# Lean tail scores for two more pairs, one matmul group moved behind its slot's unit, one decode half moved behind the tail's maximum

## The chip, the cores and the metric

The kernel runs on one core of one Trainium2 chip. The metric is the device time of one execution in microseconds. The engines are TensorE (PE; its weight loads are listed apart as PEld), VectorE (DVE), ScalarE (ACT), GpSimd (POOL) and SyncE (SP, which issues DMAs here).

## The reference

Attention with a multiplicative decay, then a mixing layer with a low-rank token mix and a feed-forward block, all in float32, for 8 batches, 8 heads, 576 tokens and 64 columns per head:

```
scores = scale * q @ k^T
cum    = cumsum(log(clip(f, 1e-4, 1)), axis=-1)
scores = where(causal, -1e9, scores + cum[:, None] - cum[None, :])
attn   = softmax(scores)            # max subtracted, sum + 1e-9
x      = attn @ v                   # heads put side by side: (8, 576, 512)
h      = x^T @ U @ V                # rank 32, over tokens
u      = x + h^T
out    = u + relu(u @ w1) @ w2      # 512 -> 2048 -> 512
```

## The kernel before

The work is cut into 32 pairs of heads (four pairs a batch) that run through a pipeline of steps. Step t has ten slots. In its slots TensorE does, in an order written out in the function `step`: the scores of pair t, the transposes of the exponentials and the value products of pair t-1, and the last value products, output transposes and rank products of pair t-2. Each slot can also take one unit of a filler list. In the step in which a batch's fourth pair is done, the units are those of the mix (`mix_units`: H, Tu, Tv); in the others they are the first half of the feed-forward block (`ffn_units`: A is a group of 12 matmuls, B of 6). After about 690 us only the second half of the feed-forward block is left.

The scores of one head of a pair are four blocks of 128 rows, S_00 to S_03 and S_10 to S_13 (head, block). The last 64 tokens of both heads are done together as "the tail", in two halves of 288 columns, St_0 and St_1 (`score_tail`). Each score goes through the same chain: TensorE writes it into a bank of PSUM, VectorE takes the masked row maximum (L439, for the tail L477), ScalarE takes the exponential out of the bank (L449, for the tail L487, named Ptl). A later score is put in the same bank, so it waits for that exponential. Pairs 0 to 5 work on plain float32 operands (L415); pairs 6 to 31 on operands that are split in two parts (L418, L419, L472, L473), which ScalarE and GpSimd make for the next pair (G, L339 to L359).

`ranks` (L715) makes Tt, nine small matmuls on the outputs xh and xl of pair t-2. It takes a bank of a pool of two, T, shared with the transposes T_10, T_11, T_12. From Tt ScalarE makes two copies (L718, L719) and VectorE one difference (L722). The outputs' split xh, xl is made on ScalarE and GpSimd (L699, L700, L701).

The feed-forward weights arrive in a packed form and are decoded piece by piece in the first steps by `decode` and `decode_words` (L76 to L93, on VectorE and ScalarE). From piece 12 on (`LATE`) a piece is decoded in two halves, and the second half is put behind a named instruction by `behind`: an order on VectorE without a wait.

In steps 1 to 6 only TensorE's order is written by hand, from step 7 on SP's too; a scheduler orders VectorE, ScalarE and GpSimd. `defer(phase, fn, n)` hands a function to the slot n slots later. `NO` is the first pair whose tail takes the mask with the decay already in it (`load_tail` L368, `lean_mask` L382), and `NF` the first with split operands. With both at 6, `join_tail` (L377, L378) never ran.

Of the kernel before, what the change touches and what calls it, by code (L numbers as in the profile page):

```python
# [36 lines left out]
NG = B + 1  # L37
NX = 3
NF = 6
NO = 6  # L40


@with_exitstack
def tile_decay_attention_moe(ctx, tc, qk, v, f, U, V, w1, w2, out):
    nc = tc.nc
# [9 lines left out]
    newest = {}  # L55

    def behind(ins, kind):
        found = newest[kind]
        for x in found if isinstance(found, tuple) else (found,):
            tc.add_manual_dep(  # L60
                ins.ins, x.ins.name,
                mybir.DependencyInfo(mybir.DependencyClass.NoSync, mybir.DependencyReason.DATA), reason=f"order behind {kind}",
            )

    def decode(raw, a, h, l, eng, rows=slice(0, 128), keep=False, sub=nc.gpsimd, low=None, halves=(0, 1)):

        lo, hi = raw[..., 0].bitcast(U32), raw[..., 1]
        af, gf = a.bitcast(F32), hi.bitcast(F32)
        if 0 in halves:
            decode_words(a, af, hi, gf, eng, keep)
        if 1 in halves:
            third = nc.vector.tensor_scalar(hi, a, -0x800000, None, op0=ALU.bitwise_and)  # L76
            if 0 not in halves:
                behind(third, "top")
            nc.vector.scalar_tensor_tensor(gf, lo, 2.0**-52, gf, op0=ALU.mult, op1=ALU.mult)
            sub.tensor_tensor(af, af, gf, op=ALU.add)  # L80
            nc.scalar.copy(h, af)
            (low or sub).tensor_tensor(l[rows], af[rows], h.bitcast(F32)[rows], op=ALU.subtract)

    def decode_words(a, af, hi, gf, eng, keep):

        if eng is nc.scalar:
            first = nc.scalar.mul(af, gf, 2.0**-112)
        else:
            first = eng.tensor_scalar(af, gf, 2.0**-112, None, op0=ALU.mult)
        if keep:  # L90
            tc.keep_in_program_order(first)
        nc.vector.tensor_scalar(hi, hi, -0x80000000, None, op0=ALU.bitwise_and)
        nc.vector.scalar_tensor_tensor(a, a, 3, hi, op0=ALU.logical_shift_left, op1=ALU.bitwise_or)  # L93
# [156 lines left out]
    def decode_w(u, halves=(0, 1)):  # L250
        load_w(u)
        raw, a = staged[u]
        if 1 in halves:
            staged[u] = None
        kind, fc = UNITS[u]
        if kind == "w1":
            h, l = (x[:, fc].rearrange("p c f -> p (c f)") for x in (w1h, w1l))
        elif kind == "w2":
            h, l = w2h[:, fc], w2l[:, fc]
        elif kind == "V":  # L260
            h, l = VV, VV
        else:
            raw = raw.rearrange("p (c r) t -> p c r t", c=NM + 1)
            a = a.rearrange("p (c r) -> p c r", c=NM + 1)
            h, l = Us[:, :, 0:RK], Us[:, :, RK : 2 * RK]
        decode(raw, a, h, l, nc.scalar, slice(96, 128) if kind == "V" else slice(0, 128), keep=True, sub=nc.vector if u not in (0, LATE) else nc.gpsimd, low=nc.vector if 0 < u < LATE else nc.gpsimd, halves=halves)
        if u == len(UNITS) - 1 and 1 in halves:
            nc.gpsimd.memset(xn[NX - 1][64:128, NM, :], 0.0)

# [7 lines left out]
    def defer(phase, fn, slots=1):  # L277
        later.setdefault(now[0] + slots, []).append((phase, fn))
# [6 lines left out]
    def run_filler():  # L285
        w, fn = filler.pop(0)
        fn()
        return w
# [73 lines left out]
    def load_tail(p):  # L362

        if not NO <= p < NP:
            return
# [4 lines left out]
    def join_tail(p):  # L370

        if not NO <= p < NF:
            return
# [6 lines left out]
    def lean_mask(p):  # L380
        if NO <= p < NP:
            nc.gpsimd.tensor_tensor(lean[:, MAIN:S], lean[:, MAIN:S], tri, op=ALU.add)  # L382
# [40 lines left out]
    def bank_s(p, name):  # L423

        scored[0] += 1
        if p < NF and scored[0] % 2:
            return psF.tile([P, 512], F32, tag="F", name=name)
        return psS.tile([P, 512], F32, tag="S", name=name)
# [31 lines left out]
    def score_tail(p, x):  # L460
        z = st[p]
        ps = bank_s(p, f"St{p}_{x}")
        cols = slice(hw * x, hw * x + hw)
        if p < NO:
            for j in range(2):
                qk_mm(ps[:, :hw], p, ATAIL[j], cols, j == 0, j == 1, j)
        elif p < NF:
            nc.tensor.matmul(ps[:, :hw], both_q, both_k[:, cols], start=True, stop=True)
        else:
            at = [slice(AOFF[j] + cols.start, AOFF[j] + cols.stop) for j in range(2)]  # L470
            for j in range(2):
                nc.tensor.matmul(ps[:, :hw], G[j][:, 0, ATAIL[j] : ATAIL[j] + P], G[j][:, 2, at[j]], start=j == 0, stop=False)  # L472
            nc.tensor.matmul(ps[:, :hw], G[1][:, 1, 0:P], G[1][:, 3, at[1]], start=False, stop=True)  # L473
        z["tl"].append(ps)

        def top():
            nc.vector.tensor_tensor_reduce(  # L477
                ps[:, :hw], ps[:, :hw], lean[:, hw * x : hw * x + hw], scale=-SCALE,
                scalar=3.0e38 if x == 0 else z["nm"][:, 8:9],
                op0=ALU.add, op1=ALU.min, accum_out=z["nm"][:, 8 + x : 9 + x],  # L480
            )

        def use():
            if x == 1:
                z["ptl"] = sb.tile([P, S], F32, tag="Ptl", name=f"Ptl{p}")
                for y in range(2):
                    newest["tail"] = nc.scalar.activation(  # L487
                        z["ptl"][:, hw * y : hw * y + hw], z["tl"][y][:, :hw], AF.Exp, bias=z["nm"][:, 9:10],
                        scale=-1.0, accum_out=z["sm"][:, 8 + y : 9 + y],
                    )  # L490

        defer(0, top)
        defer(2, use)
# [211 lines left out]
    def ranks(p):  # L705
        z = st[p]
        b, hp = z["b"], z["hp"]
        if hp == 0:
            TSb[b] = sf.tile([P, DM], F32R, tag="TS", name=f"TS{b}")
        TS = TSb[b]  # L710
        fs = slice(P * hp, P * hp + P)
        tp = psT.tile([P, 512], F32, tag="T", name=f"Tt{p}")
        for i in range(NM + 1):
            for x in (z["xh"], z["xl"])[: 2 if i < NM else 1]:
                nc.tensor.matmul(tp[0:64, 0:P], Us[:, i], x[:, i], start=i == 0 and x is z["xh"], stop=i == NM)  # L715


        defer(1, lambda: nc.scalar.copy(TS[0:64, fs], tp[0:64, 0:P]))  # L718
        defer(1, lambda: nc.scalar.copy(TS[96:128, fs], tp[0:32, 0:P]))  # L719
        defer(  # L720
            4,
            lambda: nc.vector.tensor_tensor(  # L722
                TS[64:96, fs], tp[0:32, 0:P], TS.bitcast(F32)[0:32, fs], op=ALU.subtract
            ),
        )
# [208 lines left out]
    LATE = 12  # L934
# [7 lines left out]
    def step(t):  # L942
        p = SEQ[t]
        a, c = (SEQ[t - x] if t >= x else None for x in (1, 2))
        ps_, pa, px = p is not None, a is not None, c is not None
        last, ending = t == LAST, t > LAST - 2
# [7 lines left out]
        for s in range(6 + 2 if last else SLOTS):  # L954
# [35 lines left out]
            if (t, s) in DECODES:  # L990
                u = DECODES.index((t, s))

                steps = [lambda: load_w(u + (3 if u < 6 else 2)), lambda: decode_w(u)]
                if u < LATE:
                    for fn in steps if u < 8 else steps[::-1]:
                        at(6, fn)
                else:
                    at(6, lambda: decode_w(u, (0,)))
                    defer(6, lambda: decode_w(u, (1,)), 3)
                    defer(6, steps[0], 3)  # L1000
            run_later()
            if s == 4 and ps_ and p > NF:
# [30 lines left out]
                turn_p(a, 1, s - 6)  # L1033
            if pa and s == 7:
                values(a, 0)
            if px and s == (6 if last else 8):
                ranks(c)

            if mixing:
                for _ in range(2 if t == MIX[0] and s < 3 else 1):  # L1040
                    mixing.pop(0)[1]()
                for _ in range(1 if ending else (1, 1, 2, 1, 1)[s] if s < 5 else 0):
                    if filler:
                        run_filler()
            elif len(filler) > held(t) and s in ROOM:

                ahead = sum(x >= s for x in ROOM) + len(ROOM) * (min(m for m in MIX if m > t) - 1 - t)
                credit[0] += (len(filler) - held(t)) / max(ahead, 1)
                if credit[0] > 0.999 or t > LAST - 3:
                    credit[0] = max(credit[0] - 1, 0)  # L1050
                    run_filler()
            if ps_ and s == 6:
                score(p, 1, 0)
            if last and s == 7:
# [114 lines left out]
    with tc.manual_schedule(engines={ET.PE, ET.DVE, ET.Activation, ET.SP}):  # L1169
# [12 lines left out]
        h, t = ([fn for _, fn in x] for x in (mixing[0 : NM + 1], mixing[NM + 1 :]))  # L1182
# [622 lines left out]
```

## Time and profile before

| | |
|---|---|
| time, median of 3 executions | 1185.39 us (1185.22 to 1187.29) |
| the profiled execution, its own time | 1184.63 us |
| its span, first to last instruction | 1182.9 us |
| TensorE's mean granted clock | 0.999 |
| busy: PE, PEld | 1168.8 us, 1074.3 us |
| busy: DVE, ACT, POOL | 903.0 us, 752.7 us, 594.2 us |

The span is what the views of the trace add up to. About 1.7 us of the execution's own time lie around it. The median of the three timed executions is 0.76 us above the profiled one.

### The profile page before, as it was taken

How to read it: one execution, taken by the hardware profiler on the slowest of the kernel's cores; microseconds unless marked ns; L12 is line 12 of the kernel's file. 1: busy time of each engine (PE TensorE's matmuls, PEld its weight loads, DVE VectorE, ACT ScalarE, POOL GpSimd, SP SyncE). 2: the span in 40 equal slices, each digit the busy share in tenths (PEclk: the TensorE clock that was granted, in tenths of full speed). 3: DMA queues.
4: the chain of work that ended last, by engine and by line, in shares of the span. 5: the costliest groups of instructions: out<-in, count | busy, mean ns of one | idle time of the engine just before them, and what ended most of it. 6: DMA issues, size and time to landing. Idle time of an engine off the chain costs nothing.

```text
span 1182.9 us, 24145 instructions
## 1 busy us (share of the span) xinstructions
PE 1168.8 (99%) x8348; PEld 1074.3 (91%) x8348; DVE 903.0 (76%) x2185; ACT 752.7 (64%) x2046; POOL 594.2 (50%) x668
## 2 busy tenths in 40 slices
PE   9999999999999999999999999999999999999998
PEld 5888899899999989989989987798999999999998
DVE  8987787677777677777686799967776767777675
ACT  8878786766868668867765577344454544544443
POOL 4216766547648458666563000024575555555554
PEclk9999999999999999999999999999999999999999
DMA  5754545536536536546443155352325335243411
GB/s 159 205 151 135 149 121 163 147 98 171 141 98 183 151 86 178 135 112 178 108 129 111 70 163 182 109 143 98 100 90 141 93 124 143 90 117 99 131 49 36
DMA packets 90610, 150.47 MB, mean 127 GB/s; under 512 B 12888, under 2 KB 50264, under 8 KB 88440
## 3 DMA queue, kind: packets, MB, share of 16 engines
q1 hardware_dynamic: 88856, 140.14, 40.4%
q0 software_dynamic: 1152, 8.39, 3.8%
q8 instruction: 66, 1.08, 0.4%
q14 instruction: 56, 0.46, 0.1%
q10 hardware_dynamic: 480, 0.40, 0.1%
HBM read 108.64 MB, written 35.93 MB: 122 GB/s over the span
## 4 chain that ended last, share of the span: by engine, by line
PE 85%; DVE 9%; ACT 3%; issue 1%; DMA 1%; POOL 1%; SPq 0%; DVEq 0%; POOLq 0%; ACTq 0%
PE N L1416 12%; PE B L854 11%; PE A L832 11%; PE A L1396 9%; PE B L1396 7%; PE V L642 6%; PE T L530 4%; PE S L418 3%; PE S L419 2%; PE O L1497 2%; PE B L1416 2%; PE V L607 2%; PE S L415 2%; PE Tt L715 2%; PE O L1260 1%
## 5 line engine op out<-in xcount | busy, mean ns | idle before, releaser
L208 POOL TENSOR_TENSOR hb<-xn,hb 128x256 fp32r<-128x256 f32 x136 | 111.6, 841 | 125.5 <-ACT hb L203 112.9
L449 ACT ACTIVATE P<-S,nm 128x128 f32<-128x128 f32 (+3 forms) x256 | 137.5, 539 | 58.0 <-DVE nm L439 56.0
L439 DVE CUSTOM_DVE_ANT_0 S<-S,mask 128x128 f32<-128x128 f32 (+3 forms) x256 | 125.4, 494 | 52.3 <-PE S L419 41.5
L832 PE MATMUL A<-uh,w1h 128*128 128x256 f32 (+1 forms) x384 | 119.7, 312 | 0.0
L832 PE MATMUL A<-ul,w1h 128*128 128x256 f32 (+1 forms) x384 | 113.6, 296 | 0.0
L832 PE MATMUL A<-uh,w1l 128*128 128x256 f32 (+1 forms) x384 | 113.4, 295 | 0.0
L203 ACT CAST hb<-xn 128x256 fp32r<-128x256 f32 x136 | 51.7, 404 | 84.6 <-DVE xn L1402 45.5
L339 POOL CAST G<-qk 64x576 fp32r<-64x576 f32 (+1 forms) x76 | 50.1, 668 | 89.2 <-PE S L419 56.8
L854 PE MATMUL B<-w2h,hh 128*128 128x512 f32 x216 | 88.2, 408 | 0.0
L509 DVE TENSOR_TENSOR PTl<-T,PTh 128x512 fp32r<-128x512 f32 (+1 forms) x156 | 78.1, 526 | 10.3 <-ACT PTh L506 9.9
L530 PE MATMUL T<-ident,P 128*128 128x128 f32 x544 | 85.3, 272 | 0.0
L854 PE MATMUL B<-w2l,hh 128*128 128x512 f32 x216 | 84.9, 393 | 0.0
L854 PE MATMUL B<-w2h,hl 128*128 128x512 f32 x216 | 84.7, 392 | 0.0
L358 POOL TENSOR_TENSOR G<-qk,G 64x576 fp32r<-64x576 f32 x52 | 74.7, 1437 | 10.8 <-issue 3.8
L1416 PE MATMUL N<-sw,hb 128*128 128x256 f32 x546 | 79.9, 282 | 0.0
L1416 PE MATMUL N<-b2h,hb 128*128 128x256 f32 x420 | 79.8, 282 | 0.0
L359 POOL TENSOR_TENSOR G<-qk,G 64x576 fp32r<-64x576 f32 x52 | 74.9, 1441 | 8.4 <-ACT G L339 7.5
L832 PEld LDWEIGHTS A<-uh,w1h 128*128 128x128 f32 x384 | 72.8, 190 | 0.9 <-DVE hl L837 0.4
L832 PEld LDWEIGHTS A<-uh,w1l 128*128 128x128 f32 x384 | 73.0, 190 | 0.5
L418 PE MATMUL S<-G 128*128 128x128 f32 x208 | 71.4, 348 | 2.0 <-ACT Ptl L487 0.9
L832 PEld LDWEIGHTS A<-ul,w1h 128*128 128x128 f32 x384 | 72.7, 189 | 0.0
L1416 PEld LDWEIGHTS N<-sw,hb 128*128 128x128 f32 x546 | 71.6, 190 | 0.0
(349 smaller groups left out, 3992.6 us busy)
## 6 DMA issues: line engine op xcount, KB each, us to landing
qk<-in_qk_dram SPq DMA_DIRECT2D x104, 288.0 KB
direct<-ud SPq DMA_DIRECT2D x48, 256.0 KB
sr<-in_w_dram SPq DMA_DIRECT2D x20, 512.0 KB
vr<-in_v_dram SPq DMA_DIRECT2D x32, 256.0 KB
ud<-uh SPq DMA_DIRECT2D x32, 256.0 KB
ud<-ul SPq DMA_DIRECT2D x32, 256.0 KB
accd<-ost SPq DMA_DIRECT2D x32, 256.0 KB
xn<-accd SPq DMA_DIRECT2D x8, 1024.0 KB
```

What stands on the lines that cost most here:

```text
L208: return leng.tensor_tensor(dl, src, dh.bitcast(F32), op=ALU.subtract)
L358: low = pin(el.tensor_tensor(g[oth, 2, cols], k[oth], gf[oth, 2, cols], op=ALU.subtract))
L359: last = pin(em.tensor_tensor(g[own, 1, cols], q[own], gf[own, 0, cols], op=ALU.subtract))
L418: nc.tensor.matmul(ps, G[j][:, 0, c0 : c0 + P], G[j][:, 2, cols], start=first, stop=False)
L439: ins = newest["top"] = nc.vector.tensor_tensor_reduce(ps[:, :w], ps[:, :w], mask[:, 512 - w : 512], scale=-SCALE, scalar=3.0e38, op0=ALU. ...
L449: ins = nc.scalar.activation(pt, ps[:, :w], AF.Exp, bias=z["nm"][:, col : col + 1], scale=-1.0, accum_out=z["sm"][:, col : col + 1])
L509: defer(2, lambda: nc.vector.tensor_tensor(dstl, src, dsth.bitcast(F32), op=ALU.subtract))
L530: nc.tensor.transpose(tp[:, P * x : P * x + P], z["P"][j][i][:, P * c : P * c + P], ident)
L832: nc.tensor.matmul(ps[:, :nt], wt[:, fc, c], ut[:, c, sl], start=m == 0, stop=m == 3 * NDC - 1)
L854: nc.tensor.matmul(ps, ht[:, fc, P * x : P * x + P], wt[:, fc], start=fc == 0 and m == 0, stop=fc == NA - 1 and m == 2,)
L1396: nc.tensor.matmul(ps, a[x][:, c], b[y][:, c], start=start and m == 0, stop=m == 5, skip_group_check=not start)
L1416: nc.tensor.matmul(ps[:, y], a[p_][:, P * y : P * y + P], w[q_], start=start and y == 0 and m == 0, stop=stop and y == 1 and m == 2,)
```

## The change

Three edits stand in the diff. `NO` goes from 6 to 4, so the tails of pairs 4 and 5 are one float32 matmul a half (L468, on both heads' operands side by side, `both_q` and `both_k`) in place of two (L415); GpSimd copies those operands (L377, L378), two DMAs a pair bring the mask's rows (L368) and GpSimd adds the triangle (L382). `ranks` goes from in front of slot 8's unit to behind it, in all steps but the last. The second half of the decoding of piece 13, in step 7, is deferred five slots rather than three, and is ordered behind the tail's maximum (`newest["low"]`, L477) rather than the newest maximum of a main score (`top`, L439).

```diff
-NO = 6
+NO = 4
...
-    def decode(raw, a, h, l, eng, rows=slice(0, 128), keep=False, sub=nc.gpsimd, low=None, halves=(0, 1)):
+    def decode(raw, a, h, l, eng, rows=slice(0, 128), keep=False, sub=nc.gpsimd, low=None, halves=(0, 1), after="top"):
...
             third = nc.vector.tensor_scalar(hi, a, -0x800000, None, op0=ALU.bitwise_and)
             if 0 not in halves:
-                behind(third, "top")
+                behind(third, after)
...
-        decode(raw, a, h, l, nc.scalar, slice(96, 128) if kind == "V" else slice(0, 128), keep=True, sub=nc.vector if u not in (0, LATE) else nc.gpsimd, low=nc.vector if 0 < u < LATE else nc.gpsimd, halves=halves)
+        decode(raw, a, h, l, nc.scalar, slice(96, 128) if kind == "V" else slice(0, 128), keep=True, sub=nc.vector if u not in (0, LATE) else nc.gpsimd, low=nc.vector if 0 < u < LATE else nc.gpsimd, halves=halves, after="top" if u == LATE else "low")
...
         def top():
-            nc.vector.tensor_tensor_reduce(
+            newest["low"] = nc.vector.tensor_tensor_reduce(
                 ps[:, :hw], ps[:, :hw], lean[:, hw * x : hw * x + hw], scale=-SCALE,
...
-                    defer(6, lambda: decode_w(u, (1,)), 3)
+                    defer(6, lambda: decode_w(u, (1,)), 3 if u == LATE else 5)
...
-            if px and s == (6 if last else 8):
+            if px and last and s == 6:
                 ranks(c)
...
                     credit[0] = max(credit[0] - 1, 0)
                     run_filler()
+            if px and not last and s == 8:
+                ranks(c)
             if ps_ and s == 6:
                 score(p, 1, 0)
```

On TensorE, slot 8 of step 15 stood so before (a name ends in its tile's number; A_0_5 is the slot's unit, of which the first and the last matmul are shown):

```order
L530 MATMUL T_12_4143<-ident,P_13_3879 128x128 x2
L715 MATMUL Tt_4147<-xh_4032,Us 64x128
L715 MATMUL Tt_4147<-xl_4033,Us 64x128
...
L832 MATMUL A_0_5_4157<-uh_3738,w1h 128x256
...
L418 MATMUL S_13_4187<-G_92 128x512
```

and so in the changed kernel:

```order
L530 MATMUL T_12_4153<-ident,P_13_3889 128x128 x2
L832 MATMUL A_0_5_4157<-uh_3748,w1h 128x256
...
L832 MATMUL A_0_5_4157<-ul_3749,w1h 128x256
L715 MATMUL Tt_4170<-xh_4042,Us 64x128
L715 MATMUL Tt_4170<-xl_4043,Us 64x128
...
L418 MATMUL S_13_4197<-G_92 128x512
```

Tt is now the last thing in front of the score S_13. On VectorE, in the same slot, the unit's difference (L837) stands now in front of Tt's (L722), which is still the last in front of S_13's maximum. The rows of the changed kernel:

```order
L509 TENSOR_TENSOR PTl_3919<-T_12_4153,PTh_3918 128x128
L837 SCALAR_TENSOR_TENSOR hl_0_3942<-A_0_5_4157,hh_0_3941 128x256
L722 TENSOR_TENSOR TS_3846<-Tt_4170,TS_3846 32x128
L439 ISA S_13_4197,nm_3883<-S_13_4197,mask 128x512
L439 ISA nm_3883 128x1
```

On VectorE in step 7, around the tail's second maximum, before (L76, L79 and L80 are the decode half):

```order
L477 ISA St_0_1606,nm_1474<-St_0_1606,mask 128x288
L76 TENSOR_SCALAR xn_109<-stg_1079 128x512
L837 SCALAR_TENSOR_TENSOR hl_0_1457<-A_0_2_1578,hh_0_1456 128x256
L580 TENSOR_TENSOR PT_1508<-Ty_None,PT_1508 64x128
L79 SCALAR_TENSOR_TENSOR xn_109<-xn_109 128x512
L477 ISA St_1_1637,nm_1474<-St_1_1637,mask,nm_1474 128x288
L837 SCALAR_TENSOR_TENSOR hl_0_1457<-A_0_3_1612,hh_0_1456 128x256
L80 TENSOR_TENSOR stg_1079<-stg_1079,xn_109 128x512
L509 TENSOR_TENSOR PTl_1507<-T_v,PTh_1506 128x2x2x64 x2
L509 TENSOR_TENSOR PTl_1507<-T_10_1664,PTh_1506 128x512
L439 ISA S_10_1682,nm_1474<-S_10_1682,mask 128x128
```

and in the changed kernel:

```order
L477 ISA St_0_1610,nm_1484<-St_0_1610,mask 128x288
L837 SCALAR_TENSOR_TENSOR hl_0_1467<-A_0_2_1588,hh_0_1466 128x256
L580 TENSOR_TENSOR PT_1518<-Ty_None,PT_1518 64x128
L477 ISA St_1_1641,nm_1484<-St_1_1641,mask,nm_1484 128x288
L76 TENSOR_SCALAR xn_109<-stg_1091 128x512
L837 SCALAR_TENSOR_TENSOR hl_0_1467<-A_0_3_1616,hh_0_1466 128x256
L79 SCALAR_TENSOR_TENSOR xn_109<-xn_109 128x512
L509 TENSOR_TENSOR PTl_1517<-T_v,PTh_1516 128x2x2x64 x2
L80 TENSOR_TENSOR stg_1091<-stg_1091,xn_109 128x512
L439 ISA S_10_1692,nm_1484<-S_10_1692,mask 128x128
```

The maximum of St_1 has passed L76 and L79, and the first differences of PTl and S_10's maximum have moved with it. On GpSimd, at the end of step 2 and in step 3 (a + is a row that is only there after, a - one that stood there before; qk_98 and qk_99 are the operands of pair 4):

```order
 L701 TENSOR_TENSOR xl_552<-xn_107,xh_551 128x512
+L377 COPY both_q<-qk_98 64x64
+L378 COPY both_k<-qk_98 64x576
 L521 MEMSET PT_671 64x128
-L700 TENSOR_TENSOR xh_738<-xn_107,xh_738 64x128
-L701 TENSOR_TENSOR xl_739<-xn_107,xh_738 128x512
+L377 COPY both_q<-qk_99 64x64
+L378 COPY both_k<-qk_99 64x576
 L154 MEMSET G_91 64x576
...
+L700 TENSOR_TENSOR xh_738<-xn_107,xh_738 64x128
+L701 TENSOR_TENSOR xl_739<-xn_107,xh_738 128x512
+L382 TENSOR_TENSOR mask<-mask,tri 128x64
```

The second half of xh and xl (L700, L701), which Tt of step 3 reads, stands now behind two copies that need the load of qk_99, and behind five memsets.

## Rows read from the trace of the kernel before

**Rows 1.** The page: busy time of each engine, and the chain by engine

```profile
...
PE 1168.8 (99%) x8348; PEld 1074.3 (91%) x8348; DVE 903.0 (76%) x2185; ACT 752.7 (64%) x2046; POOL 594.2 (50%) x668
...
PE 85%; DVE 9%; ACT 3%; issue 1%; DMA 1%; POOL 1%; SPq 0%; DVEq 0%; POOLq 0%; ACTq 0%
```

**Rows 2.** Waits of TensorE's weight loads: us, times, longest

```profile
...
PEld S L418 <- ACT Ptl L487: 3.5, 15, 1.1
...
PEld Tt L715 <- DVE PTl L509: 3.4, 11, 0.5
```

**Rows 3.** Fp32 tail scores of pairs 0 to 5, by form

```profile
...
L415 PE MATMUL St<-qk 128*128 128x288 f32 x48 | 13.4, 411 | 0.1
```

**Rows 4.** Timeline of step 4, TensorE and ScalarE (start, duration, engine, line)

```profile
...
68.69 1.14 PE L415 MATMUL St<-qk 128*128 128x288 f32 x4
...
70.54 0.82 PE L415 MATMUL S<-qk 128*128 128x128 f32 x4
...
70.25 0.26 ACT L449 ACTIVATION_READ_ACCUMULATOR P<-S,nm 128x1 f32 x1
```

**Rows 5.** Timeline of step 5, the same two engines

```profile
...
85.67 0.82 PE L415 MATMUL S<-qk 128*128 128x128 f32 x4
...
84.62 0.23 ACT L449 ACTIVATION_READ_ACCUMULATOR P<-S,nm 128x1 f32 x1
```

**Rows 6.** Timeline of step 3: a DMA issue, GpSimd, and Tt

```profile
...
50.52 1.18 SPq L307 DMA_DIRECT2D qk<-in_qk_dram  x2
...
51.77 0.45 POOL L700 TENSOR_TENSOR xh<-xn,xh 64x128 fp32r<-64x128 f32 x1 [6.84 <-ACT xh L699]
...
55.62 0.20 POOL L158 MEMSET G<- 128x128 f32 x1
...
60.64 0.30 PE L715 MATMUL Tt<-xh,Us 128*64 128x128 f32 x1
```

**Rows 7.** A later mask row: its DMA issue and GpSimd's use of it

```profile
...
103.38 1.14 SPq L368 DMA_DIRECT2D mask<-based  x2
...
107.14 0.32 POOL L382 TENSOR_TENSOR mask<-mask,tri 128x64 f32<-128x64 f32 x1 [0.53 <-DMA mask<-based]
```

**Rows 8.** Timeline of step 7: GpSimd, VectorE, TensorE's loads

```profile
...
122.19 1.77 POOL L208 TENSOR_TENSOR VS<-vr,VS 128x640 fp32r<-128x640 f32 x1
...
123.21 1.29 DVE L79 SCALAR_TENSOR_TENSOR xn<-xn 128x512 f32<-128x512 uint32 x1
...
124.43 0.51 DVE L477 CUSTOM_DVE_ANT_0 St<-St,mask,nm 128x288 f32<-128x288 f32 x1
...
125.67 0.19 PEld L418 LDWEIGHTS S<-G 128*128 128x128 f32 x1 [1.10 <-ACT Ptl L487]
...
128.82 0.44 PE L418 MATMUL S<-G 128*128 128x384 f32 x1 [0.36 <-ACT P L449]
```

**Rows 9.** The same line 79 in step 4

```profile
...
71.38 0.69 DVE L79 SCALAR_TENSOR_TENSOR xn<-xn 128x512 f32<-128x512 uint32 x1
```

**Rows 10.** Two of the waits of line 715's weight loads

```profile
...
191.33 0.13 PEld L715 LDWEIGHTS Tt<-xh,Us 128*64 128x64 f32 x1 [0.22 <-DVE PTl L509]
...
298.22 0.13 PEld L715 LDWEIGHTS Tt<-xh,Us 128*64 128x64 f32 x1 [0.52 <-DVE PTl L509]
```

**Rows 11.** End of step 15 and start of step 16

```profile
...
300.25 0.28 DVE L722 TENSOR_TENSOR TS<-Tt,TS 32x128 fp32r<-32x128 f32 x1 [0.26 <-ACT TS L719]
...
302.51 0.19 ACT L449 ACTIVATION_READ_ACCUMULATOR P<-S,nm 128x1 f32 x1
...
302.80 0.36 PE L418 MATMUL S<-G 128*128 128x256 f32 x1
```

**Rows 12.** End of step 10, in which a batch is mixed

```profile
...
193.63 0.59 ACT L755 COPY full<-Tu 128x512 f32<-128x512 f32 x1
...
195.25 0.19 ACT L449 ACTIVATION_READ_ACCUMULATOR P<-S,nm 128x1 f32 x1
...
195.49 0.39 PE L418 MATMUL S<-G 128*128 128x256 f32 x1
```


## The prediction

> **What bounds the kernel now.** I read the page first. TensorE is busy for 1168.8 of 1182.9 us, and the chain that ended last runs over it for 85% [rows 1]. So a gain is either TensorE work taken out or one of its idle stretches closed, and those sum to only 14.1 us. The next view is the list of waits of TensorE's weight loads, which is where a stalled TensorE shows: a matmul's load stands still before the matmul does. Two of its longest entries are touched by the diff: line 418 waiting for the exponentials Ptl (3.5 us in 15 places, the longest 1.1) and line 715 waiting for VectorE's difference PTl (3.4 us in 11 places) [rows 2]. Then I looked at the timeline around each place, to see which release would end last once the listed one is gone. That second release decides this change, because most PSUM banks are handed on with a few tenths of a us to spare.
>
> **Lean tails of pairs 4 and 5.** A tail half before is two float32 matmuls, which the trace records as four rows; a row takes 0.41 us alone [rows 3], and four in a run take 1.14 us, so one follows another after (1.14 - 0.41) / 3 = 0.24 us [rows 4]. A lean half is one matmul, two rows: 0.49 us less. Four halves make 1.95 us at most. The trace has no row of line 468; its operands have the same kind and width as those of the tail rows, so I take their spacing.
>
> How much of it stays is read from the score behind the tails. In step 4 the group of S_10 and S_11 starts at 70.54, while ScalarE finishes the exponential that S_11's bank waits for (that of S_03) at 70.25 + 0.26 = 70.51 [rows 4]. S_11 comes some 0.2 us into its group, so TensorE can come only about 0.2 us earlier before it waits there. I keep 0.2 of 0.97. In step 5 the same exponential is done at 84.62 + 0.23 = 84.85 and the group starts at 85.67 [rows 5], so S_11 has about 1.0 us of room: I keep 0.9, a little under the whole, since the scheduler moves one ScalarE copy in front. The sum is -1.1 us, the bounds -0.2 (both steps held by ScalarE) and -1.95.
>
> What the edit adds is off TensorE: four GpSimd copies and one mask add a pair, and two DMA issues a pair of 0.57 us each on SP [rows 7]. I cost it at nothing because of slack on GpSimd, with one tight place. In step 3 the copies of qk_99 now stand in front of five memsets and of L700 and L701. That load's issue ends at 51.70 [rows 6]. The nearest DMA with a visible consumer, a mask row, was used 107.14 - 104.52 = 2.6 us after its issue [rows 7], so the copies start near 54.3. The two copies I put at 0.45 (a 128-column operation on 64 partitions, [rows 6]) and 0.9 (half of the two-input operation of 640 columns, 1.77, [rows 8]); the block from L700 to the last memset took 55.82 - 51.77 = 4.05 us [rows 6]. This ends at 59.7, and Tt of step 3, which reads xl, starts at 60.64 [rows 6]: 0.9 us to spare. With a copy of the full 1.77 it is just used up, and each further 0.1 us of delay costs 0.1 us.
>
> The row of line 79 in step 7 shows what GpSimd can do to VectorE: 1.29 us with a GpSimd operation running from 122.19 to 123.96 [rows 8], 0.69 us for the same shape in step 4 with none [rows 9]. The Trainium skill, SBUF — State Buffer, section Who interferes with whom, says that a VectorE instruction with two SBUF inputs and a GpSimd instruction that reads SBUF exclude each other and that the second one waits for the first to finish. The trace agrees in size: 1.29 is 0.60 more, and GpSimd's operation ended 0.75 us after line 79 began. By that rule the new copies would hold up decode instructions of steps 3 to 5 by up to a copy each; what they delay is decoding and the tail's exponentials, whose banks are taken over two scores after S_11, so the sum would stay as it is.
>
> **The decode half in step 7.** Before, VectorE works on L79 from 123.21, and the tail's second maximum starts only at 124.43; its exponential then lets S_10 go at 125.67, after 1.10 us of waiting [rows 8]. In the new order the maximum passes L76 and L79, so it can start at 123.2, 1.2 us earlier. S_10 would then wait for almost nothing: at most 1.1 us is gained. The work does not go away, it stands behind: S_10's maximum now follows L79, the first PTl differences and L80, and S_12 takes the bank of S_10's exponential, which it already waits for at 128.82 [rows 8]. In the new order S_10's maximum has passed one difference, PTl of T_10 (about 0.7 us), and has been passed by none, but ScalarE has the G casts in front of that exponential. I put the gain that reaches S_12 at 0.5 us, between 0 (the old wait moves to S_12 whole) and 1.1.
>
> **Tt behind the unit.** Tt's bank is that of T_11, so Tt waits until VectorE has read T_11. With a unit in between (0.4 to 1.5 us of TensorE work) that wait is over, which is 3.4 us in 11 places [rows 2]: six steps that mix a batch with 0.22 each (1.3 us in all, as at 191.33), and five with a feed-forward unit (0.26, three of 0.52, as at 298.22, and 0.22; 2.0 us) [rows 10]. But now Tt's evacuation runs right in front of S_13's maximum: on ScalarE two copies, on VectorE L722 with 0.28 us [rows 11]. So the exponential of S_13 comes about 0.28 us later against TensorE than before, and its bank is the one that S_01 of the next step needs. At the end of step 15 that exponential is done at 302.51 + 0.19 = 302.70, and S_01 starts at 302.80 [rows 11]: there 0.52 us can be closed in front, and about 0.3 is kept, as it is at the other such place (step 23). The remaining three with a feed-forward unit have over a microsecond of room at S_01 and keep all, 1.0 us together. Kept: 1.6 us.
>
> In the six mixing steps S_01 already follows the exponential at 0.05 us (195.25 + 0.19 = 195.44 against 195.49) [rows 12]. There the gain of 0.22 ends at S_01 in any case, and what counts is when the exponential comes. The copy of the fourth Tu (0.59 us, [rows 12]) moves in front of the exponential of S_12, and everything behind it up to L722 and S_13's maximum comes about 0.1 us later, so I book +0.1 six times, +0.6. One more step (step 8, no wait before, 0.1 us of room at S_01) I book at +0.1. The other moved places have no wait to lose and over 1 us of room. Sum: -1.6 + 0.7 = -0.9 us; bounds -3.4 (all waits gone, nothing given back) and +2.5 (0.28 us lost at the nine places with 0.1 us of room or less, nothing kept).
>
> **Sum.** -1.1 - 0.5 - 0.9 = -2.5 us. Against the profiled execution, 1184.63, that is 1182.1; against the median, which is 0.76 above it, 1182.9. A measurement of this kernel can tell about 0.2%, 2.4 us, from no change, so the forecast lies just at that line: faster, by a hair.
>
> **Rivals.**
> *All the waits vanish.* The schedulers' order and small shifts make room where I saw none, and TensorE keeps 1.95 + 1.1 + 3.4 = 6.4 us: 1179.0; half way between my sum and this, 1181. For it: TensorE is the bound, and each edit closes a wait that the profile names. Against: the 0.03 to 0.1 us of room at S_11 of step 4 and at S_01.
> *Tt's gain comes back at S_01.* The exponential of S_13 is late by the 0.28 us at each of the nine tight places and nothing of the five is kept. Then Tt alone is +2.5 us, and with the other two edits the kernel ends at 1185.39 + 2.5 - 1.6 = 1186.3, slower than before. It decides from the point where the room at S_01 is under 0.28 us and ScalarE has no idle time in front of that exponential. For it: the margins of 0.05 and 0.10. Against: in the feed-forward steps ScalarE now gets the unit's relu earlier, which gives 0.28 us back. A half of it, 1184.6, is the likelier form.
> *GpSimd late in step 3.* The copies wait for a load that lands 2 us later than my 2.6: Tt of step 3 waits about 1.1 us, lean tails bring nothing in sum, 1184.
> *The lean tails change nothing,* because ScalarE holds both steps: 1183.8.
>
> **How the numbers follow.** My forecast, with its own range of 1181.7 to 1184.0, gets 0.50. All waits vanish: 0.18. Tt's gain comes back, in whole or half: 0.20. GpSimd late or lean tails held: 0.12. Of the first, six in ten lie beyond the 2.4 us, so faster is 0.30 + 0.18 = 0.48; slower by over 2.4 us needs the second rival and late GpSimd work together, 0.07; the rest, 0.45, is within. The range for eight in ten is 1180.2 to 1185.8: it takes in half of the first rival's extra gain and most of the second.
>
> **What would show it.** Right: six to eight records fewer on TensorE in steps 4 and 5 (four matmuls of two rows, eight in all), no wait of line 715 for PTl after step 6, no wait near 1.1 us of line 418 for Ptl in step 7, and in their place small waits of line 418 for the exponential of S_13 at the head of the step after each mixing step, about 0.3 us each. Wrong: line 715 waiting for GpSimd in step 3; those waits at S_01 larger than 0.4 us or at steps that had room; S_12 of step 7 waiting 0.9 us or more; a wait of line 415 for ScalarE in step 5.

## The result, and the profile after

The changed kernel takes 1192.77 us (median of 6 executions, 1191.13 to 1194.41) against 1185.32 us of the kernel before (6 executions): a ratio of 1.0060, 95% interval 1.0047 to 1.0073. It is slower by about 7 us. Its six executions form two groups, 1191.1 to 1191.8 us and, at a lower mean granted clock (0.997 to 0.998 against 0.999 to 1.000), 1193.7 to 1194.4 us; the median lies between them, and the profile is that of the fastest. The forecast was 1182.9 us, with a range from 1180.2 to 1185.8.

The page of the changed kernel (span and instructions; then busy time of each engine) shows less TensorE work and a longer span:

```profile
span 1189.4 us, 24159 instructions
...
PE 1167.2 (98%) x8340; PEld 1072.9 (90%) x8340; DVE 906.1 (76%) x2185; ACT 754.7 (63%) x2046; POOL 600.4 (50%) x678
```

Eight records are gone from TensorE, as forecast, and its busy time fell by 1.6 us [rows 1]. The span grew by 6.5 us, so TensorE stands idle for 8.1 us more. The list of waits of its weight loads says where (us in total, times, longest; compare [rows 2]):

```profile
PEld St L472 <- POOL G L358: 7.2, 6, 1.4
PEld S L418 <- ACT P L449: 3.8, 10, 1.3
...
PEld S L418 <- ACT Ptl L487: 2.1, 12, 0.2
```

The waits of Tt (line 715) for PTl are gone from the list, and the 1.1 us wait of line 418 for Ptl as well: both edits did what they say. In their place stands a wait that was not there before and that the prediction did not name: in six places, the tail's line 472 waits 0.7 to 1.4 us for GpSimd's line 358. These are the six steps that follow a mixing step. The start of the tail in step 11 is 0.05 us behind the kernel before (202.08 against 202.03), in step 12 it is 0.95 us behind (223.85 against 222.90).

In step 11 of the kernel before, GpSimd did this (timeline: start, duration, engine, line; line 758 casts a mixed Tu, line 759 takes its difference, lines 359 and 358 take the differences of the second head's operands of the pair whose scores run, line 339 casts for the pair after):

```profile
195.44 0.61 POOL L758 CAST uh<-full 128x512 fp32r<-128x512 f32 x1
196.01 1.29 POOL L759 TENSOR_TENSOR ul<-full,uh 128x512 fp32r<-128x512 f32 x1
197.26 1.57 POOL L208 TENSOR_TENSOR VS<-vr,VS 128x640 fp32r<-128x640 f32 x1
198.91 1.44 POOL L359 TENSOR_TENSOR G<-qk,G 64x576 fp32r<-64x576 f32 x1
200.43 1.44 POOL L358 TENSOR_TENSOR G<-qk,G 64x576 fp32r<-64x576 f32 x1
201.82 0.66 POOL L339 CAST G<-qk 64x576 fp32r<-64x576 f32 x1
202.44 1.28 POOL L759 TENSOR_TENSOR ul<-full,uh 128x512 fp32r<-128x512 f32 x1
...
202.03 0.43 PE L472 MATMUL St<-G 128*128 128x288 f32 x2
```

(the last row is the tail on TensorE, both matmuls without a wait) and in the changed kernel, with the weight load of the tail under it:

```profile
195.81 1.29 POOL L759 TENSOR_TENSOR ul<-full,uh 128x512 fp32r<-128x512 f32 x1
197.06 1.58 POOL L208 TENSOR_TENSOR VS<-vr,VS 128x640 fp32r<-128x640 f32 x1
198.59 1.31 POOL L759 TENSOR_TENSOR ul<-full,uh 128x512 fp32r<-128x512 f32 x1
199.97 1.43 POOL L359 TENSOR_TENSOR G<-qk,G 64x576 fp32r<-64x576 f32 x1
201.47 0.66 POOL L339 CAST G<-qk 64x576 fp32r<-64x576 f32 x1
202.09 1.40 POOL L358 TENSOR_TENSOR G<-qk,G 64x576 fp32r<-64x576 f32 x1
...
203.55 0.19 PEld L472 LDWEIGHTS St<-G 128*128 128x128 f32 x1 [1.39 <-POOL G L358]
```

Read line 759 and line 358 in both. The second line 759 is the split of the fourth Tu of the mixing step. It stood behind line 358, and now stands in front of line 359; the cast of line 339 has slipped in between 359 and 358 as well. GpSimd had no idle time of over 0.1 us in this stretch in either kernel, so line 358, which gives the tail its operand, ends at 203.49 instead of 201.87. The tail could start at 202.1 and starts its second matmul at 203.55. GpSimd's order is the scheduler's. Tt changed places with the fourth Tu, and that moved the Tu's copy on ScalarE forward by a few rows, and the work behind it on GpSimd forward by a place or two.

The step 7 edit in the changed kernel (VectorE's timeline, then TensorE's row of S_12; compare [rows 8]):

```profile
123.50 0.51 DVE L477 CUSTOM_DVE_ANT_0 St<-St,mask,nm 128x288 f32<-128x288 f32 x1
...
124.80 0.68 DVE L79 SCALAR_TENSOR_TENSOR xn<-xn 128x512 f32<-128x512 uint32 x1
...
126.07 1.90 DVE L80 TENSOR_TENSOR stg<-stg,xn 128x512 f32<-128x512 f32 x1
127.89 0.28 DVE L439 CUSTOM_DVE_ANT_0 S<-S,mask 128x128 f32<-128x128 f32 x1
...
129.03 0.44 PE L418 MATMUL S<-G 128*128 128x384 f32 x1 [1.05 <-ACT P L449]
```

The tail's maximum comes 0.9 us earlier than in [rows 8], in a step that starts 0.5 us later. But S_10's maximum then stands behind L80, which takes 1.90 us, and S_12 waits 1.05 us where it waited 0.36 before: over the 0.9 us that the prediction had named as a sign of being wrong.

The lean tails, steps 3 and 4 (TensorE's loads; then GpSimd's last operation in front of Tt, and Tt):

```profile
67.29 0.31 PEld L530 LDWEIGHTS T_v<-ident,P 128*128 128x128 f32 x3 [0.48 <-DVE xn L615]
...
69.64 0.30 PEld L468 LDWEIGHTS St<-both_k,both_q 128*128 128x128 f32 x2 [0.75 <-ACT P L449]
70.64 0.42 PEld L548 LDWEIGHTS T_v<-ident,Ptl 128*128 128x128 f32 x4 [0.70 <-ACT PTh L506]
...
58.90 1.61 POOL L701 TENSOR_TENSOR xl<-xn,xh 128x512 fp32r<-128x512 f32 x1
...
61.05 0.30 PE L715 MATMUL Tt<-xh,Us 128*64 128x128 f32 x1
```

A lean half in step 4 is shorter, and the time goes straight into waits for ScalarE: the second half of the tail 0.75 us for an exponential, the transposes behind it 0.70 us for a copy.

### The profile page after: what moved, and what is told of

Its sections match the earlier page's. It is cut to its first block, busy times and chain, and to the rows that moved or that the text cites. A ratio compares the mean times of both kernels' runs of the same rounds, so it can differ in the third digit from the quotient of the medians.

```text
span 1189.4 us, 24159 instructions
## 1 busy us (share of the span) xinstructions
PE 1167.2 (98%) x8340; PEld 1072.9 (90%) x8340; DVE 906.1 (76%) x2185; ACT 754.7 (63%) x2046; POOL 600.4 (50%) x678
## 3 DMA queue, kind: packets, MB, share of 16 engines
q8 instruction: 66, 1.08, 0.4%
## 5 line engine op out<-in xcount | busy, mean ns | idle before, releaser
L439 DVE CUSTOM_DVE_ANT_0 S<-S,mask 128x128 f32<-128x128 f32 (+3 forms) x256 | 125.1, 493 | 43.6 <-PE S L419 33.8
```

The costliest lines, as they stand in the source:

```text
L439: ins = newest["top"] = nc.vector.tensor_tensor_reduce(ps[:, :w], ps[:, :w], mask[:, 512 - w : 512], scale=-SCALE, scalar=3.0e38, op0=ALU. ...
```

## The experiments

Theory A, formed on the two traces: nearly the whole loss is GpSimd's order in the step after each mixing step, and the three edits by themselves do about what was forecast. Against it stood theory C, the prediction's own rival (the exponential of S_13 late at S_01), theory B (the early steps set the pace), and theory D (Tt's place among the mixing units costs by ScalarE's and VectorE's order). Each ratio is against executions of the kernel before on the same chip, whose medians were 1185.45 us (the first four runs), 1185.02 (the next four) and 1185.12 (the last four). It is not the quotient of the medians, so the two can differ by some tenths of a us.

**One edit at a time.**

```diff
-NO = 6
+NO = 4
```

> Only the lean tails of pairs 4 and 5 (the first edit). Theory A (the loss of the whole change sits in the mixing steps, on GpSimd's order, and the lean tails only fail to gain): between +0.3 and +0.8 us against the kernel before, since the start of step 6 was 0.4 us later in the changed kernel. Theory B (the early steps set the pace of all that follows): +2 us or more. The forecast's -1.1 us would be seen if the loss in steps 3 to 5 came from the other edits.

1184.95 us, ratio 0.9998 (0.9990 to 1.0007): no difference that can be told. The lean tails neither cost 2 us nor bring the forecast 1.1. In the profile TensorE is 0.7 us late before the first lean half. It is 1.2 us late at the value products behind the tails of step 4, since the waits there, like those shown above, come to more than the lean halves save. It has the full gain only in step 5.

```diff
-            if px and s == (6 if last else 8):
+            if px and last and s == 6:
                 ranks(c)
...
+            if px and not last and s == 8:
+                ranks(c)
```

> Only Tt behind its slot's unit. Theory A: +6 to +7 us, with the waits of line 472 for GpSimd's line 358 in the six steps after a mixing step as in the changed kernel (0.7 to 1.4 us each). Theory C (the prediction's rival: the exponential of S_13 comes late at S_01): +1 to +2.5 us, and no wait of line 472. The forecast: -0.9 us.

1190.73 us, ratio 1.0049 (1.0037 to 1.0061), with the six waits of line 472, 7.9 us in all. In the medians that is 5.3 us, somewhat under the 6 to 7 expected. This edit alone carries most of the loss, as theory A said; theory C's size does not fit.

```diff
-                behind(third, "top")
+                behind(third, after)
...
-                    defer(6, lambda: decode_w(u, (1,)), 3)
+                    defer(6, lambda: decode_w(u, (1,)), 3 if u == LATE else 5)
```

> Only the decode half behind the tail's maximum. Theory A and the forecast: -0.5 us, between 0 and -1.1. If GpSimd's order, which changes at one place near step 7, costs something, about 0.

1184.95 us, ratio 1.0000 (0.9991 to 1.0008): too small to be told by the times. The profile shows the step: S_10 and S_11 gain 1.1 to 1.4 us, and all but about 0.5 us of that is gone by step 9.

```diff
+            mixes = bool(mixing)
-            if px and s == (6 if last else 8):
+            if px and (s == 6 if last else mixes and s == 8):
                 ranks(c)
...
+            if px and not last and not mixes and s == 8:
+                ranks(c)
```

> Tt behind its slot's unit in the steps that do not mix a batch; in the six mixing steps it stays in front, and GpSimd's order is the same as in the kernel before. Theory A: no wait of line 472 for GpSimd, and the time falls by 0.5 to 2 us against the kernel before. Theory C: slower by 0.5 us or more, since S_01 at the tight steps 8, 15 and 23 waits for the exponential of S_13.

1183.84 us, ratio 0.9983 (0.9973 to 0.9994): faster, by 1.6 us in the medians, with the edit in fewer places. Line 472 waits for GpSimd once, for 0.2 us. The six waits of Tt that are left are those of the mixing steps:

```profile
PEld Tt L715 <- DVE PTl L509: 1.3, 6, 0.2
```

Theory C falls here: at its tight steps the edit gains. Between this run and the one with Tt behind its unit everywhere lie 6.9 us, and the only difference of the two sources is Tt's place in the six mixing steps.

**Is it GpSimd's order, or Tt's place?** The next two kernels have Tt behind its unit everywhere and change only what GpSimd does after a mixing step.

```diff
                 def parts_of():
                     nc.gpsimd.tensor_copy(dh, whole)
-                    nc.gpsimd.tensor_tensor(dl, whole, dh.bitcast(F32), op=ALU.subtract)
+                    last = nc.gpsimd.tensor_tensor(dl, whole, dh.bitcast(F32), op=ALU.subtract)
+                    if late == 2:
+                        behind(last, "lows")
+                        newest["split"] = last
...
-        pin(copy(ek2, g[own, 3, cols], k[own]))
+        third = pin(copy(ek2, g[own, 3, cols], k[own]))
+        if j == 0 and newest.pop("split", None):
+            behind(third, "lows")
```

> Tt behind its unit in all steps, as in the second edit, but in the step after a mixing step GpSimd's difference for the fourth Tu and its cast for the pair after are ordered behind the two differences of the next pair's operands (lines 358 and 359 of the kernel before), as they stood there. Theory A (it is GpSimd's order that costs): the six waits of line 472 go and the time falls from the 1190.7 us of the second edit alone to 1183.5 to 1185.5 us. Theory D (Tt's own place in the mixing steps costs, by ScalarE's and VectorE's order): it stays above 1188 us.

1183.74 us, ratio 0.9994 (0.9985 to 1.0003). In its step 11 (this kernel's lines 360 and 361 are 358 and 359, its 761 is 759):

```profile
200.33 1.44 POOL L360 TENSOR_TENSOR G<-qk,G 64x576 fp32r<-64x576 f32 x1
201.74 1.28 POOL L761 TENSOR_TENSOR ul<-full,uh 128x512 fp32r<-128x512 f32 x1
202.97 0.66 POOL L339 CAST G<-qk 64x576 fp32r<-64x576 f32 x1
...
202.20 0.43 PE L474 MATMUL St<-G 128*128 128x288 f32 x2
```

The tail runs at 202.20 with no wait, and the 7 us are back. Theory D falls: Tt is in the same place as in the slow kernel, and the traces of the two have the same order of instructions on TensorE, VectorE and ScalarE; only GpSimd's differs. This shows the cause.

The next one puts back only the cast, not the difference:

```diff
                     nc.gpsimd.tensor_tensor(dl, whole, dh.bitcast(F32), op=ALU.subtract)
+                    if late == 2:
+                        newest["split"] = True
...
+        third = pin(copy(ek2, g[own, 3, cols], k[own]))
+        if j == 0 and newest.pop("split", None):
+            behind(third, "lows")
```

> The same, but only the cast for the pair after is put back; the difference for the fourth Tu still goes ahead. Under theory A line 358 then ends 0.6 to 0.7 us earlier than in the second edit alone, so each of the six waits of line 472 falls by about that, to 0.5 to 0.8 us, and the time to 1187 us. If only the difference of the fourth Tu counted, it stays near 1190.7 us.

1187.89 us, ratio 1.0027 (1.0018 to 1.0035): the waits fall to six of 0.7 to 0.8 us (4.7 us in all), and the time falls by 2.8 us, to 0.9 us above the 1187 expected. The loss thus has two pieces, 1.3 us of line 759 and 0.66 us of line 339 in front of line 358, less the slack that line 358 had.

```profile
204.52 0.19 PEld L474 LDWEIGHTS St<-G 128*128 128x128 f32 x1 [0.80 <-POOL G L360]
```

**What is left of the edits.** The first kernel below joins two parts already shown; the second has lean tails for one pair only; the third is the whole change with the first of the two diffs above on GpSimd's order.

```diff
-            if px and s == (6 if last else 8):
+            if px and (s == 6 if last else mixes and s == 8):
...
-                behind(third, "top")
+                behind(third, after)
```

> Tt behind its unit in the steps that do not mix, and the decode half behind the tail's maximum; no lean tails. If the two add, about 1183.3 to 1183.8 us, 1.5 to 2.1 us under the kernel before.

1183.57 us, ratio 0.9987 (0.9979 to 0.9996): as expected, the two add within what can be told.

```diff
-NO = 6
+NO = 5
```

> Lean tails for pair 5 alone. If step 4 is the one that ScalarE holds and the copies and DMAs in step 3 are what delays the start of step 4, this keeps most of its 0.97 us: -0.5 to -0.9 us against the kernel before, and no delay of step 4. If the lean tail itself does not pay wherever it stands, within 0.3 us of the kernel before.

1184.43 us, ratio 0.9994 (0.9985 to 1.0003). The median is 0.6 us lower, at the expected end, but the interval holds no change. In its profile TensorE gains 0.98 us at the two lean halves of step 5 and gives 0.47 back at the next value products, for which the values land late. Step 4 starts 1.2 us late there, where no delay was expected: it comes from a wait of 1.2 us for the values of pair 2 (below). The copies for pair 5 hold VectorE only from 60 us on, in L82 (1.15 us for 0.68).

```diff
-NO = 6
+NO = 4
...
+                        behind(last, "lows")
...
+            behind(third, "lows")
```

> The whole change with GpSimd's order after the mixing steps put back as in the run before that did so. Theory A: the six waits of line 472 for GpSimd go and with them 7 us, so that this stands between 1183.5 and 1186 us. If the three edits hurt each other in another way, it stays above 1188 us.

1184.80 us, ratio 1.0007 (0.9990 to 1.0024); one execution took 1194.86. The 7 us are back with the change otherwise whole. It does not beat the kernel before, though its parts without pair 4's lean tail do (below). One likely reason, which no run singles out, is visible in its profile, in step 3 (its line 717 is 715, its 703 is 701):

```profile
62.23 0.13 PEld L717 LDWEIGHTS Tt<-xl,Us 128*64 128x64 f32 x1 [0.65 <-POOL xl L703]
```

That is the prediction's third rival in small: xl stands behind the copies for pair 4 and comes late.

```diff
-NO = 6
+NO = 5
...
+                        behind(last, "lows")
...
-                behind(third, "top")
+                behind(third, after)
```

> Tt behind its unit with GpSimd's order kept, the decode half behind the tail's maximum, and lean tails for pair 5 only: the sum of the parts that did not lose. If they add: 1183 us, 2 to 2.5 us under the kernel before; if they share one room, as the early steps may, about 1184.

1183.29 us, ratio 0.9985 (0.9976 to 0.9994). Faster than the kernel before, a little under the sum of its parts.

**A wait that came and went.** In several of these profiles TensorE waited in step 3 for the values of pair 2 (line 607). The next two kernels put that load ahead of four others on SP's queue.

```diff
-            nc.sync.dma_start(vr[64 * r : 64 * r + 64, NM], v[p, MAIN:S])
+            newest["vr"] = nc.sync.dma_start(vr[64 * r : 64 * r + 64, NM], v[p, MAIN:S])
...
-            nc.sync.dma_start(dst[0:64], src[:, x])
+            ins = nc.sync.dma_start(dst[0:64], src[:, x])
+            if p == 4 and j == 1:
+                behind(ins, "vr")
```

> The same, and the values of pair 2 are loaded ahead of the second half of pair 4's operands on SP's queue, about 3 us earlier. In most of the profiles so far TensorE waited 0.4 to 1.9 us at 56 to 58 us for that load, and in some its granted clock then fell for some us. If that wait decides: 1 to 1.5 us less than without, 1181.5 to 1182.5 us, and no run 3 us above the median.

1182.40 us, ratio 0.9975 (0.9966 to 0.9984), all ten executions between 1181.77 and 1183.33. It is the fastest kernel of this study: 2.7 us under the kernel before, 10 us under the changed one. Against the run before it, without that load ahead, it gained 0.9 us, a little less than expected, and the two intervals overlap.

> The kernel before with only that load ahead. If the wait for the values at 56 to 58 us is in most executions: 1184 to 1184.5 us, about 1 us less than the kernel before, and a narrower spread (the runs of before spread from 1184.2 to 1189.4). If it is an accident of profiled runs: no change.

1184.39 us, ratio 0.9991 (0.9983 to 1.0000), executions from 1183.93 to 1185.59, where those of the kernel before beside it went from 1184.30 to 1188.12. The gain is at the edge of what can be told; the narrower spread is as expected.

## Why the prediction was wrong

**Tt behind the unit, the mixing steps: the step that failed.** The prediction booked "+0.1 six times, +0.6" for the mixing steps, from ScalarE's and VectorE's order and the room at S_01. That part of it was right as far as it went: in the changed kernel the exponential of S_13 in step 10 ends at 195.29 + 0.19 = 195.48 and S_01 starts at 195.57, against 195.49 in [rows 12]; waits of about 0.3 us at S_01, which the prediction expected after each mixing step, are not in the trace:

```profile
195.29 0.19 ACT L449 ACTIVATION_READ_ACCUMULATOR P<-S,nm 128x1 f32 x1
...
195.57 0.36 PE L418 MATMUL S<-G 128*128 128x256 f32 x1
```

What was left out is the third engine. The copy of the fourth Tu, which the prediction saw move forward on ScalarE, feeds two GpSimd operations, and the scheduler moved these forward too, past the operands of the next pair's tail. The runs put 6.9 us in place of the 0.6: Tt moved in the mixing steps or not is 1190.73 against 1183.84. The new order could be read before any run; the prediction read GpSimd's order only in step 3, for the lean tails, and took for granted that an edit of TensorE's order leaves GpSimd's where no operand of GpSimd is named.

**Tt behind the unit, the other steps: right.** The forecast kept 1.6 us and lost 0.1; the run with Tt moved in these steps alone gave 1.6 us in the medians. The rival that the gain comes back at S_01 did not happen: in that run's profile S_01 waits 0.15 and 0.16 us at the two tight places behind steps 15 and 23, close to the 0.2 us that the forecast gave back at each.

**The decode half: right in mechanism, and in size as far as one profile tells.** S_10's wait went, S_12 took over most of it, and about 0.5 us were left by step 9 in the profile of that edit alone. What takes it back is L80 with 1.64 to 1.90 us, where the prediction counted its usual length; the times can't tell 0.5 us.

**The lean tails: a delay put at nothing.** The forecast was -1.1 us; that edit alone gave -0.5 in the medians, with an interval that holds zero. Step 5 did as forecast: in the profile TensorE gains 1.0 us at its tails (0.9 was booked) and gives 0.35 back at the value products. Step 4 was to give 0.2 and gave nothing. The step of the prediction that failed is the one on GpSimd's copies: it saw that they would hold up VectorE, and left the sum as it was because what they delay would be decoding and the tail's exponentials. In step 3 of the kernel before, two of VectorE's operations took this long:

```profile
56.09 0.43 DVE L76 TENSOR_SCALAR stg<-stg 128x512 int32<-128x512 int32 x1
...
58.19 0.15 DVE L499 TENSOR_TENSOR sm<-sm 128x1 f32<-128x1 f32 x1
```

and with the lean tails alone, beside a copy with memsets behind it, and beside L701, which the copies had pushed back:

```profile
54.92 1.06 POOL L378 COPY both_k<-qk 64x576 f32<-64x576 f32 x1
...
55.81 1.49 DVE L76 TENSOR_SCALAR stg<-stg 128x512 int32<-128x512 int32 x1
...
58.72 1.61 POOL L701 TENSOR_TENSOR xl<-xn,xh 128x512 fp32r<-128x512 f32 x1
...
59.11 1.23 DVE L499 TENSOR_TENSOR sm<-sm 128x1 f32<-128x1 f32 x1
```

From there VectorE is 1.1 us behind (its L615 starts at 61.93 against 60.79), and so are the main scores' maxima of step 4 and the exponentials that wait for them. The value products at the start of step 4 wait 0.4 us for VectorE, and the tail's second half 0.75 for an exponential. The traces show this chain, but no run removes the copies' delay and nothing else. The GpSimd rival in step 3 was real but small: 0.5 us of room in the changed kernel (60.51 against 61.05, 0.9 was forecast), a wait of 0.65 in one other.

**Size of the whole.** Lean, Tt and decode alone come to -0.5, +5.3 and -0.5 us in the medians, +4.3 together; by the ratios it is +5.6. The change was +7.4 in the medians, but from the lower group of its executions (median 1191.42) it is +6.1. The intervals of the change and of Tt alone overlap (1.0047 to 1.0073, 1.0037 to 1.0061). So whether the edits harm each other is not shown; the wait for xl in step 3 and the values' load are candidates that were not told apart.

## What to carry to other kernels

When a hand-ordered engine is changed and other engines are ordered by a scheduler, compare the order of every engine, over the whole program, and then look at each row that moved ahead of something which a busy engine waits for. A gain of a few tenths in many places can be undone by one displaced operation per repetition: here 2 us of GpSimd work ahead of an operand with 0.2 us of slack made TensorE wait up to 1.4 us in each of six steps, 7.2 us in all. A move that pays in most places may lose in sum if it is applied in all; try it apart in the steps that differ.

## What the runs showed of the hardware

The landing of a load can decide a step from one execution to the next. In the kernel with the decode edit alone TensorE waited for the values of pair 2, and then ran at a lower clock. TensorE's timeline:

```profile
58.22 1.11 PE L607 MATMUL V<-vr,PTh 128*128 128x64 f32 x7 [1.84 <-DMA vr<-in_v_dram]
```

and windows of the same kernel (busy time of PE, PEld, DVE, ACT and POOL, the granted clock, the DMA share, GB/s):

```profile
55.00:58.00 3.00, 1.37 (x11) 1.03 (x9) 2.97 (x11) 2.79 (x10) 0.82 (x3) 1.00 0.60 164
58.00:61.00 3.00, 2.78 (x16) 2.81 (x17) 2.07 (x5) 1.59 (x5) 0.00 (x0) 0.65 0.37 103
61.00:64.00 3.00, 3.00 (x16) 3.00 (x16) 0.00 (x0) 0.00 (x0) 0.00 (x0) 0.50 0.06 16
```

After a wait of 1.84 us the granted clock fell to 0.50, the lower of its two levels (1.2 GHz), while TensorE was busy again. A step that had lost 1.9 us was 5.2 us behind by its end, and the execution took 1189.43 us where the median is 1184.95. Two other profiles show a fall after shorter waits at the same place: to 0.50 after 1.08 us (Tt alone) and to 0.54 after 1.36 us (Tt in the steps that do not mix, with the decode half), both read from 60 to 62 us. Two more had waits of 1.3 and 1.5 us without a fall, so the length of this wait alone does not tell. The profile of the kernel before, on which the whole prediction was built, is one in which this load was just in time; most of the later ones were not. In the kernel before with that load ahead, the load's last issue ends at 52.80, two us earlier, and the value products start at 56.36 with no wait:

```profile
51.55 1.25 SPq L332 DMA_DIRECT2D vr<-in_v_dram  x2
...
56.36 2.34 PE L613 MATMUL V<-vr,PTh 128*128 128x64 f32 x20
```

The second is L80's 1.90 us on VectorE, an operation with two inputs in SBUF that took 0.69 us in step 4 of the kernel before. It ran from 126.07 to 127.97, and GpSimd's difference of line 359 from 125.99 to 127.42 (the row of step 4, then GpSimd's of the changed kernel):

```profile
72.58 0.69 DVE L80 TENSOR_TENSOR stg<-stg,xn 128x512 f32<-128x512 f32 x1
...
125.99 1.43 POOL L359 TENSOR_TENSOR G<-qk,G 64x576 fp32r<-64x576 f32 x1 [0.30 <-ACT G L339]
```

This fits the rule of the Trainium skill, SBUF — State Buffer, section Who interferes with whom, that the prediction weighed: the later of the two waits. The prediction looked for it only at the copies that the change adds, and took it to cost nothing there (step 3 above); here the decode half moved out of the way of one GpSimd operation and into the next.
